# Pooled attention and a spatially gated MLP on one core: the rest of one w_in block formed by GpSimd instead of TensorE, in a new order of all steps

## The chip, the core and the metric

One core of a Trainium2 chip. The metric is device time in microseconds (us) of one execution, lower is better. The engines are TensorE (PE in the views; PEld is its weight load), VectorE (DVE), ScalarE (ACT), GpSimd (POOL), and SyncE (SP), from whose queue all transfers are issued.

## What is computed

Eight batches, eight heads, 576 tokens, head width 64. Keys and values are averaged over groups of 8 tokens (72 remain), attention follows, and its output is the input of a gated MLP:

```python
k_p = k.reshape(B, H, Sp, pool, D).mean(axis=3)
v_p = v.reshape(B, H, Sp, pool, D).mean(axis=3)
scores = scale * np.matmul(q, k_p.transpose(0, 1, 3, 2))
attn = softmax(scores)
x = np.matmul(attn, v_p)            # laid out as (B, S, H*D)
h = np.maximum(x @ w_in, 0.0)       # w_in: 512 x 1024
u, v = h[..., :512], h[..., 512:]
v_n = (v - mean(v)) / sqrt(var(v) + 1e-6)
v_s = einsum('ts,bsd->btd', w_spatial, v_n) + b_spatial[None, :, None]
out = (u * v_s) @ w_out
```

All is held to single precision: TensorE multiplies in a rounded format (fp32r), so each operand is kept as a high part and a rest, and each product is three matmuls.

## The kernel before

The kernel is a set of steps, each a Python generator that issues a few instructions and yields: for batch b, `bK`, `bV` and `bQg` load and pool keys, values and queries; `bSg` is the scores and the softmax, `bTj` and `bYj` transpose the probabilities, `bPj` is attention times values, `bAhj` writes the result into xT; `bvc` is the v half of the first MLP product with its normalisation, `bB` and `bC` split it into high part and rest (`rounded`, L899 to L904: ScalarE's L901, then GpSimd's L903), `bsnd` (in batches 0 and 1) is the spatial product (its L933 stand in `product`), `bund` the u half (L1038), `boc` the output (L1067). Weights have steps of their own: `wvc` and `wuc` for the quarters of w_in's v and u halves, `woc` for w_out, `wsi` for w_spatial.

The order of all instructions on all engines is the string ORDER (L26 to L90): the loop at L1119 reads one name after the other and runs that step up to its next yield. The engines then work strictly in that order, each its own instructions, with semaphores between them. Nothing else sets the order.

A name's first occurrence may carry marks, which choose how a step is done. For a weight block (`load_f64`, L189 to L251) the transfer lands in pairs of 32-bit words (a 64-bit number each), and x, y and z are built from them: ScalarE L212, VectorE L217 to L228, and with `~` VectorE's L231 for z, without it ScalarE's L215 and GpSimd's L234; with `!` GpSimd's L222 and L223 for the sign; with `%` GpSimd's cast L237 for the high part, without it ScalarE's L239. The mark `^` chooses who forms the rest, x minus the high part plus z:

```python
241        if "^" in alt:
242            a = ps_big()
243            nc.tensor.matmul(a, lhsT=ident, rhs=x, start=True, stop=False)
244            nc.tensor.matmul(a, lhsT=ident_m, rhs=hi, start=False, stop=False)
245            nc.tensor.matmul(a, lhsT=ident_p, rhs=z, start=False, stop=True)
246            yield
247            nc.scalar.activation(lo, as_w(a), AF.Copy)
248        else:
249            nc.gpsimd.tensor_tensor(as_w(x), as_w(x), f32(hi), op=ALU.subtract)
250            yield
251            nc.gpsimd.tensor_tensor(lo, as_w(x), as_w(y), op=ALU.add)
```

`ps_big` and `ps_tr` take one of four PSUM buffers, which the transposes of the probabilities (L719, L724, L768) also use; ScalarE's copies L730, L773 and L774 give those back. Before, three blocks carry `^`: wv0, wv2 and wu1, the second quarter of the u half. With `^`, z has a tile of its own (L229), without it z is written over y.

Of the kernel before, what the change touches and what calls it, by code (L numbers as in the profile page):

```python
# [23 lines left out]


ORDER = (  # L26
    "ws4 wo1~ wo1 wv0~^ wo1 wo1 0Q0~^ 0Q0 ws4 0K^ 0K 0Q0 0Q1^ ws4 ws4 0K 0K wv0 wv0 0K 0K 0K 0Q1 0Q1 0S0 wo1 0S0 0S0 "
    "0S1 wv0 0S1 0Q3^ 0K wv2~^!% 0S0 0S1 0Q3 wv0 0S0 0K 0Q2^ 0Q3 0S1 0Q2 0S1 wv0 wo1 0Q2 0S0 wv2 wu0 0S2~ 0S2 0T0 0V "
    "wu0 0V 0S1 0S3~ 0T0 0S2 0T0 0S3 wv1 wv2 wv2 0Y0 0Y0 0V 0S3 0V 0S2 0S2 0V 0V 0T0 0T0 0T0 1Q0 wu0 wu1~^ wu1 wv2 0V "
    "1K^ wu0 wv2 wv2 0S3 0S3 wv1 wv1 wv1 wu0 wv3~ wv2 wu0 wu0 1K 0P0 0P0 0P0 0A10 0A10 1Q1 0T1 1Q0 1K 1K 0A00 0A00 1K "  # L30
    "wv1 1V^ 1K 1K wv1 wv1 0T1 1S0~ 1S0 0Y1 1V 1Q1 1S1~ 0T1 wv3 1S1 wv3 0T1 0T1 0Y1 1S0 1S0 1V wu1 1Q3 0T1 1S0 1K wv3 "
    "1S1 1V 1V 1V ws1 wu3~ 1S1 2K! ws1 ws1 wu1 wv3 wv3 2K 1S1 0P1 0P1 2K 2K 1V 0P1 1Q3 ws1 0A01 0A01 0A11 0A11 1Q2 "
    "1T0 wu2 wu3 wu3 0u00 0u00 1K 0v0 0v1 2K 0v0 1T0 2K 1Y0 wu2 0v0 1Q2 1S3 0v1 ws3 0v0 wu3 1S2~ wu2 wu3 0v1 1S3 1Y0 "
    "wu2 1T0 1T0 1T0 wu2 1T0 ws3 wu3 0v0 ws3 ws3 2Q1 2Q1 1S3 wo2~!% wu1 wu1 wo2 wo2 0v4 ws2 ws2 ws2 ws2 2Q2 0v4 ws2 "
    "wu2 wu2 wb 0v4 0v4 1S2 0v2 0v4 1S3 2Q0 0u01 wo2 ws2 1S3 0v4 1S2 0u03 0u03 0v1 0v2 wo2 0v4 0u02 0v2 0v4 0u01 1S2 "
# [12 lines left out]
    "1s02 wt wt 4S1 1s01 1s02 4S0 wt 1s12 4S0 1s13 1s03 0o1 2P1 4S1 2P1 2A01 2P1 1s03 2A01 2v0 wt 4V 4V 4V 4V 2A11 "
    "2A11 2v2 2v2 wt wt wt wt wt 3T1 0o0 1s10 1s00 wt 2v3 5K! 2v2 4Q2 1s10 1s12 1s12 2v1 0o2 0o2 3T0 2v3 2v3 wt wt wt "
    "5Q0 2v2 2v3 2v2 2v4 1s13 1s13 1o3 2v4 4S0 4Y0 2v1 3T0 wt wt 2v4 1s00 1o3 1o3 3T0 2v3 2v0 2v0 5Q0 2u01~ 1s02 2v0 "  # L50
    "4T0 wt 4Q2 6K! 1s02 2v4 3Y0 2u01 2B 2B 4Y0 2v1 2u00~ 2u00 2v1 1o1 2u10~ 2v0 2v4 2v4 2v1 2B 2v4 2B 2B 2C 2B 2v4 "
    "2v4 2C 5K 2u02 wt 1o0 2u10 1o0 1o0 2B 4V 1o2 4Q3 1o1 1o2 1o2 2u03 2B 2x0 2x1 2x1 5Q1 4V 3P0 3P0 2C 3P0 2x0 5K 2C "
    "2B 2x0 3Y1 4T0 4T0 3A00 2C 2C 2C 2x1 3A00 4S2~ 4T0 4S2 2x0 2c0 2x1 2c0 2C 2a1 2a1 2c0 2C 2d0 2c0 4Q3 5K 5K 5Q2 "
    "1o4 4S2 4S2 2d0 2u10 2u10 2u10 1o4 4S3 2u01 3T1 2d0 3T1 4S3 2d0 2u02 2a0 2a0 4S3 2c1 1o1 1o4 5K 5KT 5KT 2c1 2u00 "
    "5KT 2d1 2d1 5S0~ 2u00 4S2 4T1 5S0 4T1 4S3 4S3 2c1 2u00 2u01 2u01 2d1 2d1 2u03 5Q1 5S0 2u13 4S3 2u03 2c1 2u13 "
    "2u02 4Y1 3T1 4Y1 2u02 2u12 2u12 2u03 5S0 2u11 2u11 3A10 2u11 3A10 5S1~ 5S1 5S0 2u13 5V~ 5V 5T0 2o0 2u13 4T1 4T1 "
    "2u11 2u12 5S1 5Q2 2u12 5T0 5V 2o3 2o3 5S1 5S2~ 5S1 2o1 5S2 5S2 2o3 2o2 5Q3 3P1 3P1 3P1 3A11 3A11 2o1 3A01 2o0 "
    "5S2 5V 3v3 5Y0 3A01 3v2 2o1 3v0 3v3 3v3 5V 5V 3v2 3v1 3v3 5V 5Q3 3v2 3v3 3v2 3v0 3v2 3C 5S2 3v0 3v0 5T1 3v1 3v1 "
    "3C 3B 3B 3v1 3v4 3v4 3v4 5Y0 4T0 2o0 3v4 3v0 3v1 3u00~ 3u00 3B 6K 2o2 3u10~ 6V~ 3u10 3u01~ 4T0 4T0 3B 3x0 3x0 3B "
# [1090 lines left out]
```

## Time and profile before

| | |
|---|---|
| median of three runs | 530.9 us |
| all three | 533.1, 530.35, 530.9 us |
| the profiled execution's own time | 532.71 us |
| its span, first to last instruction | 530.9 us |
| granted clock of TensorE, mean | 0.996 |
| TensorE busy | 512.6 us (97%) |
| VectorE busy | 337.4 us (64%) |
| ScalarE busy | 266.2 us (50%) |
| GpSimd busy | 336.3 us (63%) |

The shares are averages over the whole execution; the views further down show stretches and single instructions. A matmul of full single precision, such as those with the identity, stands as two records in the trace. "Idle before" an instruction is the time for which its engine had nothing to do, and the name behind the arrow is what it waited for.

### The profile page before, as it was taken

The numbers are of one execution on the slowest core, as the hardware profiler recorded it, in microseconds if no ns is written. First come the engines' busy times: TensorE is split into PE (matmuls) and PEld (weight loads), VectorE is DVE, ScalarE is ACT, GpSimd is POOL, SyncE is SP. The second block draws the span as 40 slices with busy tenths as digits, with TensorE's granted clock in tenths as the row PEclk, the third lists the DMA queues.
The fourth block names the chain that finished last, engine by engine and source line by source line (L and its number), as shares of the span: only waits on it lengthen the run. The fifth ranks groups of instructions, "written<-read, shape, count | busy, mean of one in ns | idle before, by whom it ended". The sixth has DMA issues, their size and how long they took to land.

```text
span 530.9 us, 12197 instructions
## 1 busy us (share of the span) xinstructions
PE 512.6 (97%) x4513; PEld 440.1 (83%) x4513; DVE 337.4 (64%) x680; ACT 266.2 (50%) x868; POOL 336.3 (63%) x440
## 2 busy tenths in 40 slices
PE   3889989999999999999999999999999999999997
PEld 2657778989888898987998789878898879988996
DVE  5668997785676897864887488355545752455530
ACT  2779579747636345463535545253622433234421
POOL 4486989999996877775786467721774264135450
PEclk9989999999999999999999999999999999999999
DMA  7889937457546835546655456254210413201102
GB/s 215 265 192 281 196 97 177 111 140 143 143 96 179 194 111 133 153 137 149 174 122 103 96 124 169 78 139 126 93 42 20 114 41 94 65 0 41 40 1 99
DMA packets 135754, 64.89 MB, mean 122 GB/s; under 512 B 89616, under 2 KB 122640, under 8 KB 135696
## 3 DMA queue, kind: packets, MB, share of 16 engines
q1 hardware_dynamic: 135696, 64.12, 48.0%
q8 instruction: 35, 0.57, 0.4%
q14 instruction: 23, 0.19, 0.1%
HBM read 46.69 MB, written 17.40 MB: 121 GB/s over the span
## 4 chain that ended last, share of the span: by engine, by line
PE 90%; DVE 4%; DMA 2%; issue 1%; SPq 1%; ACT 0%; DVEq 0%; ACTq 0%
PE mm L1038 19%; PE mm L1067 19%; PE mm L933 18%; PE mm L863 16%; PE s_ps L684 3%; PE o_ps L811 3%; PE mm L875 2%; PE o_ps L804 2%; PE mm L939 2%; PE mm L938 2%; DMA st_r<-in_v 1%; PE tp L440 1%; DMA st<-in_moe_w_out 1%; DVE x L226 1%; DVE y L231 1%
## 5 line engine op out<-in xcount | busy, mean ns | idle before, releaser
L1038 PE MATMUL mm<-xT,win_h 128*128 128x288 f32 x512 | 103.7, 296 | 0.0
L903 POOL TENSOR_TENSOR lb<-vf,lb 128x512 fp32r<-128x512 f32 x50 | 66.3, 1338 | 31.2 <-ACT lb L901 25.5
L933 PE MATMUL mm<-wt,lb 128*128 128x288 f32 x552 | 85.2, 297 | 0.0
L1038 PEld LDWEIGHTS mm<-xT,win_h 128*128 128x128 f32 x512 | 82.5, 188 | 2.2 <-DVE g L998 0.4
L1028 POOL TENSOR_TENSOR gT<-g,gT 128x288 fp32r<-128x288 f32 (+1 forms) x64 | 48.6, 765 | 52.0 <-ACT gT L1025 51.9
L863 PE MATMUL mm<-win_h,xT 128*128 128x512 f32 x256 | 81.1, 398 | 0.0
L1067 PE MATMUL mm<-wout_h,gT 128*128 128x512 f32 (+1 forms) x264 | 80.4, 387 | 0.0
L933 PEld LDWEIGHTS mm<-wt,lb 128*128 128x128 f32 x552 | 76.6, 188 | 2.3 <-DVE g L1054 0.4
L1038 PE MATMUL mm<-xT,win_l 128*128 128x288 f32 x256 | 75.4, 294 | 0.0
L661 ACT ACTIVATE e<-s_ps,mx 128x72 f32<-128x72 f32 x200 | 60.9, 337 | 19.0 <-DVE mx L647 13.8
L863 PEld LDWEIGHTS mm<-win_h,xT 128*128 128x128 f32 x256 | 47.3, 188 | 12.8 <-issue 1.8
L1067 PEld LDWEIGHTS mm<-wout_h,gT 128*128 128x128 f32 x264 | 48.3, 188 | 10.3 <-issue 0.4
L851 POOL TENSOR_TENSOR st<-st,small 128x1 f32<-128x1 f32 (+1 forms) x40 | 27.8, 698 | 43.5 <-DVE st L849 43.2
L376 POOL TENSOR_TENSOR st<-st 128x512 f32<-128x512 f32 (+1 forms) x48 | 52.4, 1091 | 1.9
L1067 PE MATMUL mm<-wout_l,gT 128*128 128x512 f32 (+1 forms) x132 | 50.9, 385 | 0.0
L863 PE MATMUL mm<-win_l,xT 128*128 128x512 f32 x128 | 50.5, 395 | 0.0
L1038 PEld LDWEIGHTS mm<-xT,win_l 128*128 128x128 f32 x256 | 48.0, 188 | 0.0
L1025 ACT ACTIVATE gT<-g 128x288 fp32r<-128x288 f32 (+1 forms) x64 | 25.9, 413 | 41.4 <-DVE g L1054 20.1
L661 ACT ACTIVATION_READ_ACCUMULATOR e<-s_ps,mx 128x1 f32 x200 | 44.9, 224 | 0.0
L901 ACT ACTIVATE lb<-vf 128x512 fp32r<-128x512 f32 x50 | 31.0, 631 | 23.6 <-DVE vf L853 20.8
L693 POOL TENSOR_TENSOR e<-e,mx 128x512 f32<-128x512 f32 (+1 forms) x32 | 38.7, 1210 | 2.5
L187 DVE TENSOR_TENSOR xT<-o_ps,xT 128x576 fp32r<-128x576 f32 x32 | 23.7, 744 | 26.0 <-ACT xT L185 25.8
(179 smaller groups left out, 1007.8 us busy)
## 6 DMA issues: line engine op xcount, KB each, us to landing
st<-in_k SPq DMA_DIRECT2D x32, 256.0 KB
qt<-in_q SPq DMA_DIRECT2D x112, 72.0 KB
out<-ob SPq DMA_DIRECT2D x31, 256.0 KB
st<-in_v SPq DMA_DIRECT2D x48, 128.0 KB
xd<-X SPq DMA_DIRECT2D x48, 128.0 KB
pt<-xd SPq DMA_DIRECT2D x24, 256.0 KB
stw<-in_moe_w_in SPq DMA_DIRECT2D x8, 512.0 KB
pt_r<-xdr SPq DMA_DIRECT2D x48, 64.0 KB
```

The costliest lines, as they stand in the source:

```text
L376: eng.tensor_tensor(st[:, :, :w], st[:, :, :w], st[:, :, w:2 * w], op=ALU.add)
L661: nc.scalar.activation(em[:, h, :], sv[:, h % 2, h // 2, :], AF.Exp, bias=mx[:, h:h + 1], accum_out=sm[:, h:h + 1])
L693: nc.gpsimd.tensor_tensor(dst, src, by.unsqueeze(2).broadcast_to(list(src.shape)), op=ALU.mult)
L851: nc.gpsimd.tensor_tensor(rstd[:m], rstd[:m], neg_half[:m], op=ALU.pow)
L863: nc.tensor.matmul(a, lhsT=xT[:, i, o + c * P:o + (c + 1) * P], rhs=w[:, i, DH:], start=(i == 0 and j == 0), stop=(i == NK - 1 and j == 2))
L901: nc.scalar.activation(x[:, 0], quarter(q), AF.Copy)
L903: nc.gpsimd.tensor_tensor(x[:, 1], quarter(q), f32(x[:, 0]), op=ALU.subtract)
L933: nc.tensor.matmul(a, lhsT=x[:, h, c, ds], rhs=y[:, k, c], start=start and c == 0 and j == 0, stop=stop and c == 1 and j == 2, skip_group_ ...
L1025: nc.scalar.activation(dst[:, d, 0, at:at + m], g[:, o:o + m], AF.Copy)
L1028: nc.gpsimd.tensor_tensor(dst[:, d, 1, at:at + m], g[:, o:o + m], f32(dst[:, d, 0, at:at + m]), op=ALU.subtract)
L1038: nc.tensor.matmul(a, lhsT=x[:, i, d * P:(d + 1) * P], rhs=xT[:, i, o + ts.start:o + ts.stop], start=(i == 0 and j == 0), stop=(i == NK - ...
L1067: nc.tensor.matmul(a, lhsT=src[:, i, x, at:at + m], rhs=w[:, i, cols], start=(i == 0 and j == 0), stop=(i == ND - 1 and j == 2))
```

## The change

One mark goes: wu1 loses its `^`, so that its rest is formed by GpSimd's L249 and L251 instead of TensorE's L243 to L245 and ScalarE's L247. No other mark changes, and no code outside ORDER. All names stand in a new order, beginning with the third; the number of names is the same, 1698. Long stretches of the old order stay whole from batch 3 on (of 112, 210 and 79 names, for instance). Of the diff, the lines with wu1's mark:

```diff
@@ -24,69 +24,69 @@
 ORDER = (
-    "ws4 wo1~ wo1 wv0~^ wo1 wo1 0Q0~^ 0Q0 ws4 0K^ 0K 0Q0 0Q1^ ws4 ws4 0K 0K wv0 wv0 0K 0K 0K 0Q1 0Q1 0S0 wo1 0S0 0S0 "
...
-    "wu0 0V 0S1 0S3~ 0T0 0S2 0T0 0S3 wv1 wv2 wv2 0Y0 0Y0 0V 0S3 0V 0S2 0S2 0V 0V 0T0 0T0 0T0 1Q0 wu0 wu1~^ wu1 wv2 0V "
...
+    "ws4 wo1~ wv0~^ 0Q0~^ 0K^ wo1 wo1 wo1 0Q0 0Q1^ 0K 0K 0Q0 0Q3^ wv0 ws4 0K 0K ws4 wv2~^!% ws4 0K 0Q1 0K 0S0 0Q2^ "
...
+    "0S2 0S1 0S3~ 0V 0T0 wv0 wu0 0T0 0T0 wv3~ 0S2 0Y0 0V 0V wv2 wv2 0S3 0S3 0Y0 wu0 0S2 0S2 0V 0T0 0T0 wv1 wu0 wv2 "
+    "wu0 0S3 wv2 wv2 1Q0 0V wv1 1Q0 0T1 0P0 0P0 1K^ 0S3 wv1 wu1~ 1K wv2 wv1 wv1 1Q1 0P0 0A10 0A10 0A00 0A00 wu1 1K "
...
```

What the new order does on an engine, the diff doesn't tell; three places follow.

ScalarE in the first batch's attention, before; e is the exponentials of two groups of heads (L661), pt and pt_r their transposes, vp the pooled values, stw a staged block of w_in:

```order
L661 ACTIVATE e,mx<-s_ps,mx 128x72 x8
L663 ACTIVATE mx<-mx 128x8
L773 COPY pt<-tp 128x2x64
L774 COPY pt_r<-tp 128x64
L661 ACTIVATE e,mx<-s_ps,mx 128x72 x10
L663 ACTIVATE mx<-mx 128x10
L492 COPY vp<-mm 128x256
L730 COPY pt<-tp 128x4x4x32 x2
L730 COPY pt_r<-tp 128x4x4x32
L212 ACTIVATE x<-stw 128x512 x2
L215 ACTIVATE stw<-stw 128x512
```
and now:

```order
L730 COPY pt<-tp 128x4x4x32
L661 ACTIVATE e,mx<-s_ps,mx 128x72 x8
L663 ACTIVATE mx<-mx 128x8
L661 ACTIVATE e,mx<-s_ps,mx 128x72 x10
L663 ACTIVATE mx<-mx 128x10
L773 COPY pt<-tp 128x2x64
L774 COPY pt_r<-tp 128x64
L492 COPY vp<-mm 128x256
L730 COPY pt<-tp 128x4x4x32
L730 COPY pt_r<-tp 128x4x4x32
L212 ACTIVATE x<-stw 128x512
```
One of the two copies L730 of pt has moved ahead of both groups of exponentials, and L773 and L774 behind them.

GpSimd around the second batch's softmax, before; x_651 is the block wv3, e_666 and e_712 are probabilities, pt_p their last eight columns, win_l the rests of w_in:

```order
L249 TENSOR_TENSOR x_490<-x_490,win_h_75 128x512
L251 TENSOR_TENSOR win_l_76<-x_490,y_495 128x512
L693 TENSOR_TENSOR pt_p_691<-e_666,mx_599 128x8x8
L693 TENSOR_TENSOR e_666<-e_666,mx_599 128x512
L249 TENSOR_TENSOR x_651<-x_651,win_h_75 128x512
L251 TENSOR_TENSOR win_l_76<-x_651,y_657 128x512
L693 TENSOR_TENSOR pt_p_691<-e_712,mx_653 128x8x8
```
and now, where wv3 is x_609, and the probabilities are e_665 and e_702:

```order
L251 TENSOR_TENSOR win_l_76<-x_463,y_487 128x512
L251 TENSOR_TENSOR win_l_76<-x_376,y_454 128x4x128
L249 TENSOR_TENSOR x_609<-x_609,win_h_75 128x512
L693 TENSOR_TENSOR pt_p_749<-e_665,mx_598 128x8x8
L693 TENSOR_TENSOR e_665<-e_665,mx_598 128x512
L251 TENSOR_TENSOR win_l_76<-x_609,y_616 128x512
L693 TENSOR_TENSOR pt_p_749<-e_702,mx_661 128x8x8
```
The L249 of wv3 has moved ahead of the product with the probabilities.

GpSimd behind the pooling of the third batch's keys (kp, kr), before; x_813 is wu3 and x_881 wu2:

```order
L386 TENSOR_TENSOR kp_747<-st_763 128x128
L376 TENSOR_TENSOR st_r_780<-st_r_780 64x256
L376 TENSOR_TENSOR st_r_780<-st_r_780 64x128
L386 TENSOR_TENSOR kr_85<-st_r_780 64x128
L851 TENSOR_TENSOR st6_884<-st6_884,small_92 128x1
L249 TENSOR_TENSOR x_813<-x_813,win_h_75 128x512
L234 TENSOR_TENSOR y_936<-stw_811,y_936 128x512
L251 TENSOR_TENSOR win_l_76<-x_813,y_817 128x4x128
L249 TENSOR_TENSOR x_881<-x_881,win_h_75 128x512
L251 TENSOR_TENSOR win_l_76<-x_881,y_936 128x4x128
```
and now; x_803 is wu3, x_537 is wu1, x_895 is wu2:

```order
L386 TENSOR_TENSOR kp_769<-st_777 128x128
L249 TENSOR_TENSOR x_803<-x_803,win_h_75 128x512
L251 TENSOR_TENSOR win_l_76<-x_803,y_814 128x4x128
L376 TENSOR_TENSOR st_r_783<-st_r_783 64x256
L376 TENSOR_TENSOR st_r_783<-st_r_783 64x128
L386 TENSOR_TENSOR kr_85<-st_r_783 64x128
L851 TENSOR_TENSOR st6_850<-st6_850,small_92 128x1
L249 TENSOR_TENSOR x_537<-x_537,win_h_75 128x512
L251 TENSOR_TENSOR win_l_76<-x_537,y_717 128x4x128
L234 TENSOR_TENSOR y_958<-stw_818,y_958 128x512
L249 TENSOR_TENSOR x_895<-x_895,win_h_75 128x512
L251 TENSOR_TENSOR win_l_76<-x_895,y_958 128x4x128
```
wu3's two instructions stand ahead of the pooling of the keys' last columns (st_r), and wu1's two, which GpSimd did not have, follow ahead of wu2's.

## Rows read from the trace of the kernel before

**Rows 1.** The page, part 1: busy time, share of the span, instructions

```profile
PE 512.6 (97%) x4513; PEld 440.1 (83%) x4513; DVE 337.4 (64%) x680; ACT 266.2 (50%) x868; POOL 336.3 (63%) x440
```

**Rows 2.** Waits of TensorE: who waited for whom, total, times, longest (us)

```profile
PE tp L622 <- DVE y L231: 8.7, 1, 8.7
PE mm L303 <- DVE wt L314: 1.2, 1, 1.2
```

**Rows 3.** Windows: stretch, busy time of each engine (instructions), granted clock, DMA share, GB/s

```profile
core 0: us, PE busy (x) PEld busy (x) DVE busy (x) ACT busy (x) POOL busy (x), PEclk, DMA share, GB/s
0.00:32.00 32.00, 19.46 (x332) 15.40 (x332) 20.93 (x37) 17.47 (x63) 16.48 (x27) 1.00 0.84 231
32.00:36.00 4.00, 3.73 (x16) 1.69 (x16) 1.96 (x5) 3.81 (x8) 2.23 (x5) 0.57 0.92 250
60.00:72.00 12.00, 10.61 (x151) 8.10 (x151) 11.83 (x19) 8.26 (x21) 11.68 (x11) 1.00 0.66 133
72.00:514.00 442.00, 442.00 (x3627) 385.11 (x3627) 281.79 (x586) 216.88 (x710) 284.70 (x378) 1.00 0.43 108
514.00:531.00 17.00, 13.85 (x74) 11.68 (x72) 0.92 (x2) 3.53 (x7) 2.20 (x3) 0.98 0.23 77
```

**Rows 4.** Timeline, TensorE: start, us, line, operation [idle before <-releaser]

```profile
32.27 2.05 PE L243 MATMUL mm<-x,ident_p 128*128 128x512 f32 x2 [1.04 <-ACT pt L730]
...
35.11 0.94 PE L804 MATMUL o_ps<-pt_r,vr 32*128 32x288 f32 x8
...
47.20 2.00 PE L489 MATMUL mm<-st_r,four 128*128 128x64 f32 x16
...
63.19 1.12 PE L243 MATMUL mm<-x,ident_p 128*128 128x512 f32 x2
...
64.61 0.40 PE L875 MATMUL mm<-win_h,xT 128*128 128x512 f32 x1
```

**Rows 5.** Timeline, ScalarE

```profile
31.54 1.08 ACT L730 COPY pt<-tp 128x512 f32<-128x512 f32 x2
...
45.26 0.63 ACT L239 ACTIVATE win_h<-x 128x512 fp32r<-128x512 f32 x1
```

**Rows 6.** Instructions by line, GpSimd: count, busy us, mean ns, idle before

```profile
L251 POOL TENSOR_TENSOR win_l<-x,y 128x512 fp32r<-128x512 f32 x5 | 6.8, 1356 | 0.3
L249 POOL TENSOR_TENSOR x<-x,win_h 128x512 f32<-128x512 f32 x5 | 6.5, 1310 | 0.0
```

**Rows 7.** Timeline, GpSimd

```profile
46.74 0.30 POOL L693 TENSOR_TENSOR pt_p<-e,mx 128x64 f32<-128x64 f32 x1 [4.11 <-DVE mx L667]
...
48.48 1.45 POOL L249 TENSOR_TENSOR x<-x,win_h 128x512 f32<-128x512 f32 x1
...
63.93 1.30 POOL L234 TENSOR_TENSOR y<-stw,y 128x512 f32<-128x512 f32 x1
...
67.78 1.34 POOL L251 TENSOR_TENSOR win_l<-x,y 128x512 fp32r<-128x512 f32 x1
...
73.10 1.08 POOL L851 TENSOR_TENSOR st<-st,small 64x1 f32<-64x1 f32 x2 [0.62 <-DVE st L849]
...
75.17 1.39 POOL L693 TENSOR_TENSOR pt_p<-e,mx 128x64 f32<-128x64 f32 x3 [0.43 <-DVE mx L667]
...
86.83 1.41 POOL L851 TENSOR_TENSOR st<-st,small 128x1 f32<-128x1 f32 x1 [0.25 <-DVE st L849]
...
90.86 1.28 POOL L903 TENSOR_TENSOR lb<-vf,lb 128x512 fp32r<-128x512 f32 x1
```

**Rows 8.** Timeline, TensorE, the first spatial step

```profile
92.15 1.86 PE L933 MATMUL mm<-wt,lb 128*128 128x288 f32 x12
93.84 0.29 PE L938 MATMUL mm<-r_h,vt 128*128 128x288 f32 x1
```

**Rows 9.** VectorE: the normalising L853, in the timeline and by its line (ns min/median/max)

```profile
64.04 3.96 DVE L853 TENSOR_SCALAR vf<-vf,st 128x512 f32<-128x512 f32 x1
...
L853 DVE TENSOR_SCALAR vf<-vf,st x32: 498/546/3956, 64.0 to 483.6; 128x512 f32<-128x512 f32 x32
```

**Rows 10.** Timeline of SP's queue

```profile
41.54 3.31 SPq L614 DMA_DIRECT2D qt<-in_q  x4
```

121 rows, old and new, of the table ORDER are left out of this document.

## The prediction

> **What bounds the kernel now.** I read the page first: of the profiled execution's span of 530.9 us TensorE is busy 512.6 [rows 1]. So at most 18.3 us are not matrix work, and the question is where they lie. The list of TensorE's waits answers it [rows 2]: 8.7 us at the very start, before the first operand is there, then one of 1.2 us and some shorter ones. The windows by stage [rows 3] place them: from 0 to 32 us TensorE is busy 19.5 of 32, from 60 to 72 it is busy 10.6 of 12, from 72 to 514 it is never idle, and in the last 17 us it is busy 13.85, the rest being the last result on its way out. So from 72 us on, time is the sum of the matrix work; an order of steps can win only before that, and can lose anywhere. The same table shows the second limit: from 60 to 72 us VectorE is busy 11.83 of 12 and GpSimd 11.68 of 12. This is the stretch into which the change puts GpSimd work. One more thing to see there is the clock: between 32 and 36 us the granted clock is 0.57, in the other windows 0.98 to 1.00.
>
> **What the change takes from TensorE.** The block wu1 forms its rest no longer with the three matmuls of L243 to L245. In the trace they stand three times; wu1's are those at 63.19, and the next step starts at 64.61 [rows 4], so 1.42 us of TensorE's time go. The same three at 32.27 last until 35.11, 2.84 us, at half speed: those belong to wv2 and stay. L247's copy leaves ScalarE (0.6 us), which is busy 8.3 of 12 there [rows 3]; I count that as nothing.
>
> **What the new order gives TensorE early.** In front of wv2's L243 at 32.27, behind the pooling of the first values (L489), there is a wait of 1.04 us, put down to ScalarE's L730 [rows 4]. That is the release of a PSUM buffer: two L730 copy the transposed probabilities out, and stand behind eighteen exponentials, at 31.54 [rows 5]. In the new order one of the two L730 copies stands ahead of the exponentials, and the buffer is free when L489 ends. That wait goes, 1.04 us. What could be late next there is GpSimd's cast of wv2, which L244 reads; the rows show no wait of L244 for it, so I take the whole 1.04 and keep 0 as the other end. The slow clock from 32 to 36 came after TensorE had been idle 12.5 of the first 32 us; with less idle just before it, it may not come, which would give another 1.42 (2.84 against 1.42 for the same three matmuls), or it may come a little later. I take 0. So TensorE on its own account arrives 1.42 + 1.04 = 2.46 us earlier at 92 us.
>
> **What the change adds to GpSimd.** L249 and L251 on a w_in block took 1310 and 1356 ns on average [rows 6], so 2.67 us more. They go in where GpSimd now works without a pause, between 46.74 and 72 us. Its idle time up to the place that counts is, row by row [rows 7], 4.11 us before 46.74, then 0.62 before 73.10, 0.43 before 75.17, 0.25 before 86.83: after 46.74 only 1.30 us are left to take up 2.67. The place that counts is the second L903 (90.86 + 1.28 = 92.14), which splits the operand of the first spatial step. TensorE starts that step at 92.15; its twelve L933 take until 93.84 [rows 8], and the second six, from 93.0, want that operand. So GpSimd is 0.86 us ahead of TensorE now.
>
> In the new order GpSimd does wv3's L249 before the softmax product that starts at 46.74 instead of after it, in the 4.11 us of idle time; its operand from ScalarE is ready at 45.26 + 0.63 = 45.9 [rows 5], so some 1.0 us of work leaves the full stretch (bounds 0 and the 1.45 us that this L249 took [rows 7]). The second L903 then ends at 92.14 + 2.67 - 1.30 - 1.0 = 92.5. It would be ready at 93.5 if the early L249 brings nothing, and up to 1.0 earlier than 92.5 if the softmax feeding it comes earlier with TensorE's 1.04. TensorE cannot start its second six products before that. Now they start at 93.0, so the gain at this place is 93.0 - 92.5 = 0.5 us, between -0.5 and +1.5, and not the 2.46 that TensorE alone would have. The rest turns into a new wait of TensorE for L903, of 1 to 2 us. I take the upper half, a gain of 1.0, because the softmax that feeds GpSimd at 46.74 hangs on TensorE's scores, which come earlier with the wait that goes.
>
> **VectorE.** Its work is the same, except that z of wu1 is written over y. But its time is not only its own. L853 at 64.04 took 3.96 us, where its median is 0.546, while GpSimd went from one instruction into the next, four of them from 63.93 to 67.78 [rows 7, 9]; TensorE waited 1.2 us at L303 for the L314 behind it [rows 2]. More GpSimd work in this stretch can make more of that.
>
> The Trainium skill, page "SBUF — State Buffer", section "Who interferes with whom", says that the two engines share one port pair under an exclusive lock, and that the second fully blocks for a whole instruction. By that rule the two new instructions could hold VectorE up once each, 2.67 us together; L853's row agrees with it in kind.
>
> **The queues.** On SP the last load of the second batch's values (L479) goes behind four loads of q (L614 at 41.54, 3.31 us of issue) [rows 10]. TensorE reads those values at 47.20 [rows 4]. Bounds: no cost, or the 1.04 us won before it is waited away here; this is why a gain of 1.0 at GpSimd's place is not 1.5. Behind 93 us all steps keep their matmuls, and TensorE was never idle up to 514 us [rows 3], so the new order has nothing to gain there; I cost it at 0, covered by that backlog of matrix work, and at up to +0.5 if one operand comes late. In the last 17 us the same final two steps stand at the end: 0.
>
> **Sum.** -1.0 us. The profiled execution took 532.71 us, 1.81 more than its span, and would take 531.7; the median of the runs shown is 530.9, equal to that span, and I give the forecast against it: **529.9 us**, own range 529.4 to 531.4.
>
> **Rivals.**
> - *TensorE's gains arrive in full.* GpSimd's queue turns out not to be what the first spatial step waits for, because its instructions run shorter when VectorE is elsewhere. Then -1.42 - 1.04, and the 1.2 us at L303 [rows 2] goes too, since the new order has another transpose of w_spatial and the values' tail (L875) around it: -3.7, 527.2 us; with full speed from 32 to 36 us, 525.8. For it: each wait has its row. Against it: GpSimd's 1.30 us of idle time for 2.67 us of work.
> - *The matmuls leave in front of a wait.* They end at 64.61, and four microseconds later TensorE waits for VectorE's L314 anyhow [rows 2]; 1.42 us less work makes that wait longer by 1.42. With the early gain lost at the load on SP, nothing changes: 530.9. Against it: L875 and L301 around this wait are reordered.
> - *Slower: VectorE is held up by GpSimd.* One more normalising L853 blocked as the one at 64.04 costs 3.96 - 0.55 = 3.41 us, and the L901 and L903 behind it wait for it. The second L903 then ends at 92.5 + 3.4 = 95.9, and TensorE, which wants it at 93.0, is 2.9 late: 533.8 us. It decides from the moment that this L903 ends after 93.0. For it: 98% busy on both engines from 60 to 72 us. Against it: the median of its 32 instances is 0.546, that one being the longest [rows 9].
>
> **Chances.** Forecast 0.48, full gains 0.28, no change 0.12, slower 0.12. A measurement of this kernel can tell about 0.5%, 2.65 us, from no change: below 528.25 is faster, above 533.55 slower. Of the full gains 0.25 lie below that, of the forecast's low end 0.02: faster 0.27. Of the slower case 0.10 and of late operands behind 93 us 0.02: slower 0.12. Same: 0.61. The range goes from 526.8, in the lower part of the full gains, to 533.2, just under the slower case; some 0.1 is left out on either side.
>
> **What would show it.** L243 to L245 stand for two blocks instead of three; L249 and L251 on w_in stand six times instead of five. The wait at L243 for L730 is gone. A new wait of TensorE stands at L933 for GpSimd's L903, 1 to 2 us, near 90 us. From 93 to 514 us TensorE has no idle time. I am wrong if TensorE has no wait for GpSimd and starts the first spatial step before 90.5 (full gains), or if waits of more than 1 us stand behind 110 us (the order, not the block, then sets the time).

## The result, and the profile after

The changed kernel took 537.8 us (median of four runs, 536.55 to 538.48) against 530.6 us for the kernel before beside it: a ratio of 1.0112, 95% interval 1.0091 to 1.0134. That is slower by 1.1%, outside the range given, with the opposite sign. The profiled execution has a span of 536.7 us, 5.8 more than that of before. TensorE's busy time is the same to 0.1 us [rows 1], although one block's three matmuls are gone, so other matmuls stand a little longer in the views; the new 5.8 us are idle time:

```profile
PE 512.6 (96%) x4509; PEld 439.5 (82%) x4509; DVE 338.2 (63%) x680; ACT 264.9 (49%) x867; POOL 335.5 (63%) x442
```

The list of TensorE's waits (who waited for whom; total, times, longest, in us) says for what. Before, the longest behind the start was 1.2 us, for VectorE [rows 2]; now four of the five longest are for transfers (DMA):

```profile
PE tp L622 <- DMA qt<-in_q: 9.6, 2, 9.3
PE tp L440 <- DMA st_r<-in_k: 2.2, 1, 2.2
PE mm L484 <- DMA st<-in_v: 1.1, 1, 1.1
PE mm L1038 <- ACT ob L1071: 1.1, 1, 1.1
PE mm L489 <- DMA st_r<-in_v: 1.1, 1, 1.1
```

The windows of the same stretches as [rows 3], and the one between them from 36 to 60 us, place the loss. The first row is of the kernel before, where that window was not shown; the others are of the kernel after:

```profile
36.00:60.00 24.00, 22.93 (x327) 18.09 (x323) 19.98 (x34) 16.23 (x62) 18.98 (x20) 1.00 0.99 235
```
```profile
0.00:32.00 32.00, 20.21 (x334) 15.73 (x334) 19.03 (x38) 17.66 (x64) 15.71 (x26) 1.00 0.85 224
32.00:36.00 4.00, 3.57 (x39) 1.87 (x40) 2.81 (x5) 3.44 (x7) 2.86 (x6) 1.00 0.91 266
36.00:60.00 24.00, 18.50 (x281) 14.01 (x278) 17.51 (x29) 16.14 (x62) 16.37 (x17) 1.00 0.81 199
60.00:72.00 12.00, 10.18 (x157) 8.12 (x157) 9.69 (x19) 6.46 (x18) 11.29 (x12) 1.00 0.89 216
72.00:514.00 442.00, 440.63 (x3595) 382.40 (x3595) 287.00 (x588) 216.21 (x707) 284.94 (x375) 1.00 0.43 109
```

TensorE is ahead until 36 us: in this execution the clock stays at full speed where it was 0.57, and the early wait is gone. Then it loses 4.4 us in one window. Its timeline (start, us, line; idle before) shows both halves, to be read beside [rows 4] and [rows 8]:

```profile
31.32 1.08 PE L243 MATMUL mm<-x,ident_p 128*128 128x512 f32 x2
32.83 0.50 PE L244 MATMUL mm<-win_h,ident_m 128*128 128x512 f32 x1 [0.43 <-POOL win_h L237]
...
33.93 0.77 PE L804 MATMUL o_ps<-pt_r,vr 32*128 32x288 f32 x8
...
39.09 0.69 PE L440 MATMUL tp<-pairs,st_r 128*64 128x64 f32 x16 [2.19 <-DMA st_r<-in_k]
...
47.24 1.94 PE L484 MATMUL mm<-st,pairs 128*64 128x256 f32 x14 [1.15 <-DMA st<-in_v]
50.29 2.00 PE L489 MATMUL mm<-st_r,four 128*128 128x64 f32 x16 [1.11 <-DMA st_r<-in_v]
...
95.62 1.59 PE L933 MATMUL mm<-wt,lb 128*128 128x288 f32 x10
```

L804 starts 1.18 us earlier than before (33.93 against 35.11), L489 3.09 later (50.29 against 47.20), the first spatial step 3.47 later (95.62 against 92.15). SP's queue shows what has moved. Ahead of the loads that TensorE waits for stands a second block of w_in, 512 KB (L201 at 22.70; before, it came at 30.11, behind the keys), and L479 now stands behind L614, at 45.60 instead of 40.81:

```profile
22.70 0.61 SPq L201 DMA_DIRECT2D stw<-in_moe_w_in  x1
23.41 5.33 SPq L614 DMA_DIRECT2D qt<-in_q  x4
28.79 3.18 SPq L433 DMA_DIRECT2D st<-in_k  x2
32.01 0.47 SPq L203 DMA_DIRECT2D stw<-in_moe_w_in  x1
32.58 1.15 SPq L447 DMA_DIRECT2D st_r<-in_k  x2
...
41.52 3.98 SPq L614 DMA_DIRECT2D qt<-in_q  x4
45.60 1.90 SPq L479 DMA_DIRECT2D st_r<-in_v  x1
```

The issue of a load can take longer behind others: the two L433 took 3.18 us here, behind that block and four loads of q, and 1.02 in the kernel before. GpSimd has its two instructions more, at the durations of [rows 6]:

```profile
L251 POOL TENSOR_TENSOR win_l<-x,y 128x512 fp32r<-128x512 f32 x6 | 7.9, 1320 | 0.2
L249 POOL TENSOR_TENSOR x<-x,win_h 128x512 f32<-128x512 f32 x6 | 7.6, 1274 | 3.7 <-ACT win_h L239 3.7
```

**One table for all kernels.** Every span divides at two places of TensorE's timeline that all kernels have: the second L811 of the first batch (50.59 us before) and the first L933 (92.15 before). A is the time up to that L811, B from there to L933, C from L933 to the end of the span. The kernel before has A 50.59, B 41.56, C 438.75. Differences to it, in us, one profiled execution each, and the ratio of the times of all runs with its interval:

| kernel | A | B | C | ratio |
|---|---|---|---|---|
| after | +2.88 | +0.59 | +2.33 | 1.0112 (1.0091 to 1.0134) |
| e1 block alone, old order | +0.93 | +2.36 | 0.0 | 1.0086 (1.0057 to 1.0114) |
| e2 new order, block on TensorE | +0.19 | +0.99 | +2.72 | 1.0104 (1.0079 to 1.0129) |
| e3 after, loads in old order | -0.80 | -0.08 | +2.18 | 1.0055 (1.0034 to 1.0076) |
| e4 144 names new | +1.96 | -1.86 | 0.0 | 1.0030 (1.0010 to 1.0050) |
| e5 e3 with X behind vt | -0.68 | -0.10 | +0.58 | 1.0033 (1.0008 to 1.0059) |
| e6 305 names new, loads old | -0.77 | +0.15 | +0.12 | 1.0025 (1.0002 to 1.0049) |
| e7 144 names new, loads old, block on TensorE | +0.96 | -1.86 | -0.10 | 0.9982 (0.9967 to 0.9997) |
| e8 e1 with wu2 behind L314 | -1.65 | +1.17 | 0.0 | 1.0038 (1.0023 to 1.0053) |
| e9 old order, loads new | +4.23 | -0.75 | -0.08 | 1.0083 (1.0058 to 1.0109) |
| e10 after, two w_in loads old | -1.74 | -0.13 | +2.17 | 1.0072 (1.0047 to 1.0097) |
| e11 after, values' rest ahead | -0.77 | +1.40 | +2.17 | 1.0074 (1.0051 to 1.0098) |
| e12 e6 with block on TensorE | +3.17 | +0.35 | +0.08 | 1.0055 (1.0029 to 1.0080) |
| e13 e7 with block on GpSimd | -0.24 | +0.12 | -0.08 | 1.0035 (1.0004 to 1.0066) |
| e14 e7 with wv3 behind the keys' rest | +1.90 | -1.89 | -0.11 | 1.0003 (0.9975 to 1.0030) |

C repeats to 0.1 us wherever its order is the old one, and lies at +2.17 to +2.72 where it is wholly the new one. A does not repeat: e6 and e12 have the same instructions and loads up to some 58 us but for wu1's block, and differ by 3.9 us there; the runs of one kernel spread by 1 to 8 us. B depends on A: in e4, e7 and e14 TensorE is 1 to 2 us late at the end of A and makes up 1.9 in B. So A is judged by the ratios, C by the profiles, and B by both.

The granted clock adds to this. Of 89 executions of the kernel before whose mean clock is on record, 54 have 0.999 or 1.000 and a median time of 531.0 us; the other 35 have 0.990 to 0.997 and a median of 532.4. The profiled one (0.996) is of the second kind, so its window at 0.57 is not a property of the old order, and its A is some 1.4 us longer than one at full speed (an estimate from the 2.84 against 1.42 us of the same three matmuls [rows 4]). The four executions of the changed kernel have 0.999, 1.000, 0.993 and 0.994.

### The profile page after: what moved, and what is told of

The parts are those of the page before. It is cut to its first block, busy times and chain, and to the rows that moved or that the text cites. A ratio compares the mean times of both kernels' runs of the same rounds, so it can differ in the third digit from the quotient of the medians.

```text
span 536.7 us, 12201 instructions
## 1 busy us (share of the span) xinstructions
PE 512.6 (96%) x4509; PEld 439.5 (82%) x4509; DVE 338.2 (63%) x680; ACT 264.9 (49%) x867; POOL 335.5 (63%) x442
## 4 chain that ended last, share of the span: by engine, by line
PE 82%; DMA 6%; SPq 5%; DVE 3%; POOL 1%; ACT 1%; issue 1%; ACTq 0%; DVEq 0%; POOLq 0%
PE mm L933 17%; PE mm L1038 17%; PE mm L1067 17%; PE mm L863 15%; PE s_ps L684 3%; PE o_ps L811 3%; PE mm L875 3%; SPq L614 2%; DMA st<-in_v 2%; PE o_ps L804 2%; DMA qt<-in_q 2%; PE mm L938 2%; PE mm L939 2%; DMA st<-in_k 1%; DMA st<-in_moe_w_out 1%
## 5 line engine op out<-in xcount | busy, mean ns | idle before, releaser
L1038 PE MATMUL mm<-xT,win_h 128*128 128x288 f32 x512 | 103.7, 296 | 1.1 <-ACT ob L1071 1.1
L903 POOL TENSOR_TENSOR lb<-vf,lb 128x512 fp32r<-128x512 f32 x50 | 66.5, 1341 | 39.5 <-ACT lb L901 35.6
L1038 PEld LDWEIGHTS mm<-xT,win_h 128*128 128x128 f32 x512 | 82.7, 188 | 3.9 <-ACT ob L1071 1.4
L933 PE MATMUL mm<-wt,lb 128*128 128x288 f32 x552 | 84.9, 297 | 0.0
L1028 POOL TENSOR_TENSOR gT<-g,gT 128x288 fp32r<-128x288 f32 (+1 forms) x64 | 47.5, 750 | 57.8 <-ACT gT L1025 57.6
L863 PE MATMUL mm<-win_h,xT 128*128 128x512 f32 x256 | 81.1, 398 | 0.0
L933 PEld LDWEIGHTS mm<-wt,lb 128*128 128x128 f32 x552 | 76.8, 188 | 2.4 <-DVE g L1054 0.4
L1038 PE MATMUL mm<-xT,win_l 128*128 128x288 f32 x256 | 75.3, 294 | 0.0
L661 ACT ACTIVATE e<-s_ps,mx 128x72 f32<-128x72 f32 x200 | 61.1, 339 | 16.1 <-DVE mx L647 10.7
L863 PEld LDWEIGHTS mm<-win_h,xT 128*128 128x128 f32 x256 | 47.1, 188 | 13.0 <-issue 2.6
L863 PE MATMUL mm<-win_l,xT 128*128 128x512 f32 x128 | 50.6, 395 | 0.0
L851 POOL TENSOR_TENSOR st<-st,small 128x1 f32<-128x1 f32 (+1 forms) x40 | 26.3, 662 | 36.2 <-DVE st L849 36.0
L1038 PEld LDWEIGHTS mm<-xT,win_l 128*128 128x128 f32 x256 | 48.0, 188 | 0.0
L1025 ACT ACTIVATE gT<-g 128x224 fp32r<-128x224 f32 (+1 forms) x64 | 25.8, 414 | 41.5 <-DVE g L1054 24.1
L661 ACT ACTIVATION_READ_ACCUMULATOR e<-s_ps,mx 128x1 f32 x200 | 45.0, 225 | 0.0
L185 ACT ACTIVATE xT<-o_ps 128x576 fp32r<-128x576 f32 x32 | 20.3, 649 | 33.7 <-PE o_ps L811 26.5
```

The source lines that it names most:

```text
L661: nc.scalar.activation(em[:, h, :], sv[:, h % 2, h // 2, :], AF.Exp, bias=mx[:, h:h + 1], accum_out=sm[:, h:h + 1])
L851: nc.gpsimd.tensor_tensor(rstd[:m], rstd[:m], neg_half[:m], op=ALU.pow)
L863: nc.tensor.matmul(a, lhsT=xT[:, i, o + c * P:o + (c + 1) * P], rhs=w[:, i, DH:], start=(i == 0 and j == 0), stop=(i == NK - 1 and j == 2))
L903: nc.gpsimd.tensor_tensor(x[:, 1], quarter(q), f32(x[:, 0]), op=ALU.subtract)
L933: nc.tensor.matmul(a, lhsT=x[:, h, c, ds], rhs=y[:, k, c], start=start and c == 0 and j == 0, stop=stop and c == 1 and j == 2, skip_group_ ...
L1025: nc.scalar.activation(dst[:, d, 0, at:at + m], g[:, o:o + m], AF.Copy)
```

## Experiments

Theory Q: the order costs the time, that of the loads and that of the steps behind 93 us. Theory G: GpSimd's two new instructions cost it. The diffs show the names of ORDER around each edit.

**e1, the block alone.**

```diff
- wu0 wu1~^ wu1
+ wu0 wu1~ wu1
...
- 1S2~ wu2
+ 1S2~ wu1 wu1 wu2
...
- wo2~!% wu1 wu1 wo2
+ wo2~!% wo2
```

> The old order with the block alone moved: wu1's rest is formed by GpSimd's L249 and L251 (put just ahead of wu2's first VectorE step), all else stands as before. Theory Q (the order of loads on SP's queue in the first 60 us costs the time, and the later order some more): the block itself costs about nothing, 529.5 to 532 us against 530.6 before. Theory G (GpSimd's two instructions of 2.67 us make the first spatial step late, as rival three of the prediction has it): 533 to 537 us, with a wait of TensorE for L903 or L891 between 85 and 110 us.

Measured: 535.7 us, 1.0086. Theory G's size, but not its place. TensorE's longest waits are at 68 to 71 us:

```profile
PE mm L863 <- DVE wt L314: 1.7, 1, 1.7
PE mm L301 <- DMA st<-in_moe_w_spatial: 1.5, 1, 1.5
```

VectorE's timeline shows where L314 was held: wu1's y must now live until L251 has read it, only two such buffers exist, and wu2's L228 waits for one:

```profile
62.02 2.19 DVE L226 SCALAR_TENSOR_TENSOR x<-stw,x 128x512 uint32<-128x512 uint32 x1
65.39 1.51 DVE L228 TENSOR_SCALAR y<-x 128x512 uint32<-128x512 uint32 x1 [1.18 <-POOL win_l L251]
...
69.69 0.68 DVE L314 TENSOR_TENSOR wt<-mm,wt 128x512 fp32r<-128x512 f32 x1
```

So the block costs in B, not by L903 at the spatial step. At these places TensorE was idle 1.39 us in the kernel before (0.24 at L301, 1.15 at L303) and is idle 3.16 now: the 1.42 us of matmuls leave in front of a wait, as the prediction's second rival had it, and VectorE's queue adds to it. Some 1.6 us of B's +2.36 come from the clock behind these waits, granted at 0.65 from 70 to 74 us:

```profile
70.00:74.00 4.00, 3.58 (x10) 2.86 (x11) 4.00 (x8) 1.33 (x5) 3.92 (x3) 0.65 0.39 64
```

The same twelve L863 take 4.46 us there, 2.87 in the kernel before. All six executions of e1 have a mean clock of 0.990 to 0.994.

**e8, the same with wu2's steps behind L314**, to take that wait out:

```diff
- wu1 wu2 wu3
+ wu1 wu3
...
- 1Y0 wu2 1T0
+ 1Y0 1T0
...
- 1T0 wu2 1T0
+ 1T0 1T0
...
- ws3 2Q1
+ ws3 wu2 wu2 wu2 2Q1
```

> The block alone in the old order, as in the first run, with wu2's VectorE step (L217, L226, L228), ScalarE's L239 and GpSimd's L234 of wu2 moved behind VectorE's L314 that TensorE waits for. If the 4.5 us of that run come from VectorE's queue, whose L228 waits for the y buffer that wu1's L251 now holds: the wait of 1.7 us at L863 for L314 goes and the slow clock behind it too, 531 to 533 us. If GpSimd's 2.67 us of work themselves make the first spatial step late: 534.5 to 536.5 as in that run.

Measured: 533.5 us, 1.0038, between the two. The wait at L863 went, the clock stayed at 1.00 in B, and 2.5 us came back (0.48%), 1.2 of them in B; but B is still 1.17 longer than in the kernel before. A wait of 3.29 us stands at 70.37 now, for ScalarE's L312. ScalarE's queue had stood 3.73 us at L239 for wu2's x, and the L311 just ahead of that L312 waits 1.58 for VectorE's L314, which stands behind wu2's steps and another L217:

```profile
70.37 0.54 PE L1038 MATMUL mm<-xT,win_h 128*128 128x288 f32 x2 [3.29 <-ACT raw_r L312]
```
```profile
66.09 0.64 ACT L239 ACTIVATE win_h<-x 128x512 fp32r<-128x512 f32 x1 [3.73 <-DVE x L226]
...
69.71 0.49 ACT L311 ACTIVATE wt<-mm 128x384 fp32r<-128x384 f32 x1 [1.58 <-DVE wt L314]
```

With either of the two places tried for the block in the old order, TensorE waits in the stretch from 60 to 72 us [rows 3]; other places were not tried.

**e2, the new order without the block.**

```diff
- wv1 wu1~ 1K
+ wv1 wu1~^ 1K
```

> The new order, with wu1's rest formed by TensorE's L243 to L245 as before. Theory Q: the order carries all of the loss, and TensorE has 1.42 us more matrix work: 537.5 to 540 us. Theory G: with the block back on TensorE the loss goes, 530 to 533 us.

Measured: 536.7 us, 1.0104, a little under what theory Q gave. The order carries the loss; with the block back on TensorE nearly all of it is still there, and theory G falls as the main cause. By the ratios (1.0104 and 1.0112, their intervals overlapping) the block on GpSimd makes no difference in the new order. B is 0.40 longer than in the changed kernel, but A ends 2.7 us earlier, so this does not show what the block's 1.42 us are worth.

**e3, the changed kernel with its loads in the old order.** Only steps that issue transfers move:

```diff
- 0Q0 0Q1^ 0K 0K
+ 0Q0 0K 0Q1^ 0K
...
- 0T0 wv3~ 0S2
+ 0T0 0S2
...
- 0P0 1K^
+ 0P0 wu1~ 1K^
...
- wv1 wu1~ 1K
+ wv1 wv3~ 1K
...
- wv3 1Q3 0T1 1V 1S1
+ wv3 1V 1Q3 0T1 1S1
```

> The changed kernel with four steps moved that only issue transfers, so that SP's queue issues its loads of the first 60 us in the order of before: the second load of keys' rest (L447) ahead of q (L606), wv3's w_in block (L201) behind the second batch's first keys, wu1's block (L203) ahead of them, the rest of the second batch's values (L479) ahead of q (L614). Computation stands as in the changed kernel. Theory Q: the waits of TensorE at L440 (2.2), L484 (1.1) and L489 (1.1 us) for transfers go, the first spatial step starts at 92 to 93 us instead of 95.6, and the time is 533.5 to 535.5 us. Theory G: the waits may go, but the time stays within 1 us of 537.8. If the order of the computing engines, not of the loads, makes TensorE late, also 537 to 538.5.

Measured: 534.0 us, 1.0055; 0.57%, some 3.0 us, come back, as theory Q had it. Every computing engine has the instructions of the changed kernel in the same order. The first L933 starts at 91.27, 0.88 earlier than before, and the wait at L489 is gone; those at L440 and L484 are not, so the loads are still near the edge. GpSimd's L903 for the second six products of that step starts at 90.45:

```profile
PE mm L484 <- DMA st<-in_v: 1.2, 1, 1.2
PE mm L1038 <- ACT ob L1071: 1.1, 1, 1.1
PE s_ps L684 <- DVE qT L634: 1.1, 1, 1.1
PE tp L440 <- DMA st_r<-in_k: 0.9, 1, 0.9
```
```profile
90.45 1.28 POOL L903 TENSOR_TENSOR lb<-vf,lb 128x512 fp32r<-128x512 f32 x1
```

**e9, the reverse: the kernel before with only SP's queue in the new order.** All computing engines keep their instructions and their order:

```diff
- 0K^ 0K 0Q0 0Q1^ ws4
+ 0K^ 0Q1^ 0K 0Q0 ws4
...
- 0T0 1Q0 wu0 wu1~^
+ 0T0 wv3~ 1Q0 wu0 1K^ wu1~^
...
- 0V 1K^ wu0
+ 0V wu0
...
- wu0 wv3~ wv2
+ wu0 wv2
...
- 1S0 1V wu1 1Q3 0T1
+ 1S0 1Q3 1V wu1 0T1
```

> The kernel before, with only SP's queue in the new order: the three places where the changed kernel issues its loads otherwise in the first 60 us; every computing engine has the same instructions in the same order. If the order of loads alone makes TensorE late, as taking it out of the changed kernel gave back 0.57 % (3.0 us): a ratio of 1.004 to 1.007 to the kernel before, with waits of TensorE for transfers at L440, L484 or L489 of 2 to 4 us together. If loads only hurt beside the new computing order (which wants them earlier): 0.999 to 1.002.

Measured: 535.7 us, 1.0083: 4.4 us, more than expected, from the order of loads and nothing else (four moved load steps). The waits expected at L440, L484 and L489 hardly show (0.3 us at L489). Here wu1's block, issued at 31.54 behind the keys, held ScalarE and then VectorE, and the transposes of q behind it came late:

```profile
38.56 0.43 DVE L217 TENSOR_SCALAR x<-x 128x512 uint32<-128x512 uint32 x1 [6.06 <-ACT x L212]
...
42.20 0.20 DVE L635 STREAM_TRANSPOSE pt_q<-qt 128x64 f32<-128x64 f32 x1
```
```profile
42.42 1.16 PE L684 MATMUL s_ps<-kT,qT 64*64 64x72 f32 x32 [2.27 <-DVE pt_q L635]
```
```profile
40.00:44.00 4.00, 1.73 (x39) 1.24 (x41) 2.83 (x7) 3.89 (x10) 3.61 (x3) 0.82 1.00 315
44.00:48.00 4.00, 3.23 (x76) 2.75 (x80) 2.44 (x5) 3.03 (x19) 2.68 (x3) 0.50 0.69 124
```

Behind the wait the granted clock was 0.50 for a window, half speed, and all six executions of e9 have a mean clock of 0.990 to 0.994. So here the late load cost more than the wait of 2.27 us.

**e10 and e11, one part of the loads each.** Of e3's diff, e10 has the pieces on wv3's and wu1's blocks, e11 the last one, on the values' rest:

```diff
- 0T0 wv3~ 0S2
+ 0T0 0S2
...
- 0P0 1K^
+ 0P0 wu1~ 1K^
...
- wv1 wu1~ 1K
+ wv1 wv3~ 1K
```
```diff
- wv3 1Q3 0T1 1V 1S1
+ wv3 1V 1Q3 0T1 1S1
```

> The changed kernel with two of the four load steps put back: wv3's w_in block (L201) behind the second batch's first keys, wu1's (L203) ahead of them. If the 512 KB of wv3 ahead of q and the keys are what makes them late: most of the 3 us come back, ratio 1.006 to 1.0085 to the kernel before, the wait at L440 for the keys' rest below 1.2 us. If the values' rest (L479) behind q decides: 1.010 to 1.012, with the wait at L440 still 2 us.

> The changed kernel with one load step put back: the rest of the second batch's values (L479) ahead of q (L614). The step of the prediction that bounded its cost at 1.04 us: the wait at L489 (1.1 us) goes, ratio 1.0085 to 1.010 if it counts in full, 1.011 to 1.012 if TensorE only waits elsewhere.

Measured: 1.0072 and 1.0074. Each brings some 2 us back by the middle values; the intervals overlap with each other and just with that of the changed kernel. By its middle value L479 alone costs about twice the upper bound of 1.04 us that the prediction gave it, but with intervals that overlap 1.04 us is not excluded for it alone. In e10 the wait at L440 fell to 0.5, in e11 it stayed at 1.7 while that at L489 went. L489's wait is no clean sign of L479's place, though: in e10 it fell as well, with L479 still behind L614:

```profile
PE mm L489 <- DMA st_r<-in_v: 0.2, 1, 0.2
```

The two gains add up to more than e3's 3.0 us, so they are not shares of it; the fourth moved load, q ahead of the first keys' rest, was not run alone. (e11's B of +1.40 has a stretch of slow clock in it, 0.86 from 60 to 72 us.)

**e5, the wait at L1038.** On top of e3 one transpose of batch 4's probabilities goes behind batch 2's vt:

```diff
- 2u03 4T0 2B
+ 2u03 2B
...
- 2v4 1o1
+ 2v4 4T0 1o1
```

> The kernel of the run with the loads in the old order, with one VectorE instruction moved: the transpose L738 of batch 4's probabilities (X<-e) goes behind L907 and L891 of batch 2 (vt), all else the same. If the wait of 1.1 us of TensorE at L1038 for ScalarE's L1071 comes from L891 standing behind that L738, which waits 3.7 us for GpSimd's L693: the wait goes, 532.6 to 533.3 us against 534.0. If L1071 is late for another reason: 533.8 to 534.3 with the wait in place.

The chain that it is to break stands in e3's timelines of VectorE and ScalarE (in the changed kernel the same, 4.4 us later): L738 waits for GpSimd, L891 stands behind it, and L1071 behind L891:

```profile
198.66 0.71 DVE L738 STREAM_TRANSPOSE X<-e 128x512 f32<-128x512 f32 x1 [3.71 <-POOL e L693]
...
200.84 0.70 DVE L891 TENSOR_TENSOR vt<-vv,vt 64x512 fp32r<-64x512 f32 x1
```
```profile
201.63 0.59 ACT L1071 COPY ob<-mm 128x512 f32<-128x512 f32 x1 [3.58 <-DVE vt L891]
```

Measured: 532.8 us, 1.0033, and in e5 L1071 starts at 199.25. TensorE's wait is gone and C falls from +2.18 to +0.58:

```profile
199.25 0.59 ACT L1071 COPY ob<-mm 128x512 f32<-128x512 f32 x1 [1.00 <-DVE vt L891]
```

One instruction in the wrong place on an engine that is 63% busy cost 1.6 us in the profiles, 1.2 by the middle values of the ratios.

**e4 and e6, the front new and the rest old.** e4 takes the new order's first 144 names, with wu1's mark as before, e6 its first 305 with the loads of e3; the old order follows. At the two joints, against the changed kernel:

```diff
- 1V 1V 1V ws1 ws1 wv3 1S0 0P1
+ 1V 1V 1V ws1 wu3~ 1S0 2K! ws1
...
```
```diff
- 0v4 2S2~ 1T1 1T1 1T1 0C 1Y1 1T1
+ 0v4 2S2~ 1T1 0C 1Y1 0C wo3% 2S0
...
```

> The first 144 names in the new order (to about 58 us), all later ones in the old order, with wu1's block on TensorE as before. Theory Q: the front carries the 2.9 to 3.5 us that TensorE is late at 55 to 92 us, so 533 to 535 us. If the loss lies in the later order alone (behind 93 us), 530 to 531.5 us. Theory G: as before, 530 to 531.5.

> The first 305 names (to about 100 us) in the new order with the loads in the old order and wu1's block on GpSimd, all later names in the old order. If the later order carries its 2.2 us behind 100 us (a wait of 1.1 and more changes between steps): the first spatial step starts at 91 to 91.5 us, from there to the end 438.8 us as in the kernel before, so 531.3 to 532.3 us as one execution and 0.5 to 1 us below the kernel before. If the loss behind 93 us is a consequence of the block or of the front: 533.5 to 534.5.

Measured: 1.0030 and 1.0025. e4 is a little faster than expected; e6 was to be 0.5 to 1 us below the kernel before and is 1.3 above it. C is that of before in both, so its 2.33 us belong to the names behind 305. e4's B is 1.86 shorter: where TensorE comes late to 51 us with the old names behind, it finds everything ready (12.00 of 12 us busy from 60 to 72) and catches up.

**e7, e12, e13: the block in and out of mixed orders.** e7 is e4 with the pieces of e3's diff; e12 is e6 with the first line pair below; e13 is e7 with the second, and with wu1's last two steps and wu2's placed as in e1 and e8.

```diff
- 0P0 wu1~ 1K^
+ 0P0 wu1~^ 1K^
```
```diff
- 0P0 wu1~^ 1K^
+ 0P0 wu1~ 1K^
...
- ws3 2Q1
+ ws3 wu2 wu2 wu2 2Q1
```

> The first 144 names in the new order with the loads in the old order, all later names in the old order, wu1's block on TensorE as before: the run with the new front, with its loads put back. If the loads carried what that run lost (1.5 us): 530 to 531.2 us, the wait at L440 for the keys' rest below 1 us. If the front's computing order lost it, or its slow clock from 40 to 48 us comes whatever the loads: 532 to 533.

> The run with the first 305 names new, loads old and the later order old, with wu1's block back on TensorE (L243 to L245). If the block on GpSimd costs what its 1.42 us of TensorE time save, or more: 0.998 to 1.001. If it saves TensorE time here: 1.003 to 1.006.

> The run with 144 new names and the loads in the old order (ratio 0.9982), with wu1's block on GpSimd and wu2's steps behind L314 as in the old order's second run of the block. If the block is worth its three matmuls where no load is late: 0.995 to 0.997. If GpSimd's 2.67 us make the first spatial step as much later as TensorE is earlier: 0.998 to 1.000. If the block costs what it cost in the old order (1.004): 1.001 to 1.003.

Measured: e7 530.55 us, 0.9982, the one kernel whose interval lies below that of before, by 0.03% to 0.33%. Against e4 the loads give back 0.48%. In its profile the wait at L440 is 2.2 us, though, not below 1, and what is won against before is won in B. Eleven of e7's twelve executions have a mean clock of 0.999 or 1.000, against 54 of 89 of the kernel before, so part of its lead may be the clock. e12 was slower than e6 (1.0055), as a saving by the block would have it; but their intervals overlap, and in the profiles A makes the difference, and B only 0.20 (+0.35 against +0.15). TensorE is idle 1.81 us in B with the block on GpSimd and 0.64 with it on TensorE, as if the matmuls left in front of waits; but e12 enters B 3.9 us later, which alone can shorten waits, so the cause is not shown. e13 was slower than e7 (1.0035), as in the old order, and there the intervals do not overlap.

**e14, one load of e7 moved.**

```diff
- wv1 wv3~ 1K wv2
+ wv1 1K wv3~ wv2
```

> The run with 144 new names and the loads in the old order (0.9982), with one load moved: wv3's w_in block (L201, 512 KB) behind the keys' rest (L447) on SP's queue, all computing engines as there. If the wait of 2.15 us at L440 comes from those 512 KB ahead of the keys' rest: the wait falls below 1 us, 0.994 to 0.997. If it comes from the loads of q ahead of it (L614, 5.8 us of issue): the wait stays at 1.5 to 2.2 us, 0.997 to 1.000.

Measured: 1.0003. The wait at L440 is gone, so the 512 KB ahead of it were its cause; but TensorE, which is at L484 earlier than in e7, waits there for the next loads, and the time does not fall:

```profile
43.57 0.62 PE L484 MATMUL mm<-st,pairs 128*64 128x256 f32 x2 [0.48 <-DMA st<-in_v]
45.87 3.52 PE L484 MATMUL mm<-st,pairs 128*64 128x256 f32 x14 [1.67 <-DMA st<-in_v]
```

## Why the prediction was wrong

- **What the change takes from TensorE, 1.42 us.** Two blocks instead of three have L243 to L245, as said. But no run shows the 1.42 as a gain that is clear of the noise: in the new order the ratios of e2 and the changed kernel are the same, and in the old order and behind 144 new names the block on GpSimd is slower (e1, e8, e13). In e1 the idle time behind the matmuls grows from 1.39 to 3.16 us. That is the second rival, given 0.12; for this term it was right.
- **What the order gives early, 1.04 us and the clock.** Right in part: L243 has no wait, but 0.43 of it comes back at L244 for GpSimd's cast L237, the end that the text named and put at 0. The window from 32 to 36 us has full clock, for which the text took nothing; most executions of the kernel before have no such slow window either, so it is not shown to come of the order. L804 starts 1.18 earlier, and this is lost 5 us later at L440.
- **What GpSimd's 2.67 us cost.** The forecast was a gain of 1.0 us at the first spatial step and a new wait at L933 for L903. With the loads put back (e3) the gain is 0.88, but there is no such wait: L903 starts at 90.45 and ends at 91.73, not at 92.5, and TensorE, worked out as 2.46 early, is only 0.88 early. L903's end lies inside the text's bounds, 91.5 to 93.5. That 0.88 is near the forecast's 1.0 is luck: an error on each side. In the old order the block costs 2.36 or 1.17 us in B (e1, e8), by VectorE's and ScalarE's queues (wu1's y kept longer, L314 and L312 behind wu2's steps) and, in e1, 1.6 by the clock behind the waits. In the new order VectorE has no wait for L251 in that stretch.
- **VectorE.** The slower rival, one more L853 blocked, did not come: the longest of the 32 L853 of [rows 9] took 1.5 us in the changed kernel, not 3.96. By the Trainium skill, page "SBUF — State Buffer", section "Who interferes with whom", VectorE and GpSimd fully block each other only where VectorE's instruction uses the port pair that they share, so the two new instructions could each have blocked it; in the changed kernel, behind 60 us, no wait of TensorE for VectorE exceeds 0.25 us.
- **The queues: the step that failed.** The text looked at one move on SP, L479 behind four L614, and bounded it between "no cost" and "the 1.04 us won before it is waited away here". e11 gives some 2 us for it by the middle values, not clear of 1.04 by itself. And the list of moves was incomplete: the w_in block ahead of q and keys, wu1's block behind the keys, and q ahead of the keys' rest were not costed; with wv3's and wu1's blocks back some 2 us more return (e10). All four together cost 3.0 us (e3), or 4.4 us in the old order (e9), three to four times the bound. The bound took the gain just won as the most that could be lost; but a load that comes late costs until it is there, and TensorE's own earlier arrival does not count against it.
- **Behind 93 us: the second step that failed.** "The new order has nothing to gain there; I cost it at 0 ... and at up to +0.5". It measured +2.33, in other executions of that order 2.17 to 2.72: 1.6 of it one chain through L738, L891 and L1071 (e5); the rest, 0.6 to 1.1, no run took apart. With the loads and the names behind 305 put back, 0.25% of the 1.12% is left (e6). That TensorE was never idle in the old order says nothing of a new one; no backlog covers a wait in TensorE's own queue.
- **The test named in the text held:** "waits of more than 1 us ... behind 110 us (the order, not the block, then sets the time)". It stands at 206 us.

What stays open: why the clock fell to half speed in some executions and not in others. The changed kernel was busy 1.81 of the 4 us from 36 to 40, with full clock before and after; e7 was busy 2.05 of the same 4 us, and the clock was 0.50 in the next window. The same kernel takes either course from one execution to the next. Nor is it settled what A is worth to better than about 1 us, since its loads vary from one execution to the next.

## What to carry to other kernels

Where a change reorders everything, take each engine's queue in turn, the transfer queue first, and list every row that has changed its neighbours; what stands ahead of a load that a busy engine will read is a term of the sum, with no upper bound taken from the gain beside it. Work taken from the bound engine counts only if no wait follows it. To separate order from work, put only the transfers back, or only the last part of the order: a span cut at two or three common instructions shows at once in which part the time went, as long as a late start of one part, which can shorten the next, is kept in mind. Look at the granted clock of many executions before one window of a single profile becomes a term of the sum.

## What was not expected of the hardware

With all computing engines unchanged, four moved load steps on SP's queue cost 4.4 us of 531 (e9). The issue itself can take longer behind others: the two L433 of the second batch's first keys took 2.55 to 3.18 us in the five profiles that have wv3's 512 KB ahead of them and of q (the changed kernel, e2, e4, e9, e11), and 1.02 to 1.41 in the eleven others; what holds the issue is not shown. Making one load earlier need not gain: the wait taken from L440 in e14 came back at L484.
